# Keeping two PSUM banks open from attention to the end, in a kernel of windowed attention and two expert layers

## The chip, the cores and the metric

One core of one Trainium2 chip. The metric is the time of one execution on the device in microseconds (us); the median over the runs shown is what kernels are compared by.

## What is computed

The reference, cut to what matters (B=2, H=8, S=768, D=64; 4 sinks, window 128; 1536 tokens, model width 512):

```python
scores = scale * np.matmul(q, k.transpose(0, 1, 3, 2))
keep = is_sink | in_window
scores = np.where(keep, scores, -1e9)
a = softmax(scores)
x = np.matmul(a, v)                      # to [1536, 512]
h = x @ w_in                             # d_ff 2048
g = h * np.tanh(softplus(h))
x = g @ w_out
for e in range(4):                       # 4 experts, width 1024
    out += p[:, e:e+1] * (np.maximum(x @ w1[e], 0) @ w2[e])
```

## The kernel before

**Attention.** `banded` runs 24 items (batch, block of 256 queries, pair of heads). An item computes scores `sc` on TensorE, masks and maximises them on VectorE (line 234), exponentiates on ScalarE (238), scales on GpSimd, transposes on TensorE (`tp`, `ts`), and multiplies with `v` (`pv`); `evac_x` (184, 185) writes the result as the pair `xh`, `xl`, whose sum it is.

**Expert layers.** `Experts` cuts each layer's hidden width into units of 512: four units of the first layer (`kind` 0), then two per expert. `stream` goes over units and chunks of tokens. For each chunk `layer1` makes four tiles `h` (f = 0 to 3, 128 hidden values each) of twelve matmuls (four slices of 128 by three products of high and low parts); `mish` turns each into the pair `gh`, `gl`: four steps on ScalarE (552 to 555), then VectorE (556), ScalarE (557), VectorE (558, 559), ScalarE `gh` (89), GpSimd `gl` (97). The bank of `h` is read up to line 559. `layer2` makes four tiles `o` (d = 0 to 3), also of twelve matmuls, copied or added into `acc` (510 to 512). The chunks of the first unit hold 256, 256, 512 and 512 tokens; the last two are called the middle chunk (tokens 512 to 1023) and the last chunk (1024 to 1535) below. A chunk's `layer2` is interleaved with the next chunk's `layer1`.

**Attention and experts overlap.** From the sixth item on (`LAG`) each item is followed by one step of `stream`, and weight parts are converted on VectorE (`split_double`, 116 to 124) beside it. The eight banks of PSUM are dealt out by pools. During attention: one bank for `h`, one for `o`, three for `sc`, two for `tp` and `ts`, one for `pv`. At `first.close()` all eight are given back, and `psum(ctx, 3, 3, 2)` opens three for `h`, three for `o` and two for `r` (an intermediate of `mish`, which lies in `gl` as long as there is no such pool). Which tile was asked for under which pool is fixed by the Python order: the middle chunk's four `h` come from the attention phase's one-bank pool, the last chunk's from the new pool.

**Order.** The order of instructions on each engine is set when the program is built, by a scheduler that looks at dependencies and at free buffers; it does not change at run time, and an engine takes its instructions in that order. In the rows of the order and in the text tiles bear the program's numbers: h_1526, h_1624, h_1794, h_1959 are the middle chunk's f = 0 to 3; h_2099, h_2127, h_2169, h_2211 are the last chunk's in the kernel before, and h_2097, h_2125, h_2167, h_2209 the same four in the changed one. o_2155, o_2197, o_2239, o_2253 (before) and o_2153, o_2195, o_2237, o_2251 (changed) are the middle chunk's outputs. Line numbers from 404 on are larger by up to 11 in the changed kernel: 552 to 559 become 563 to 570, 510 becomes 521, 477 becomes 488, 504 becomes 515.

Of the kernel before, what the change touches and what calls it, by code (L numbers as in the profile page):

```python
# [9 lines left out]
F32 = mybir.dt.float32  # L10
# [5 lines left out]
PSUM = bass.MemoryType.PSUM  # L16

P = 128
# [18 lines left out]
class Ring:  # L37


    def __init__(self, tiles):  # L40
        self.tiles, self.n = tiles, 0
# [52 lines left out]
def split(c, hi, lo, src, eng_hi, eng_lo):  # L94

    copy(c, eng_hi, hi, src)
    eng_lo.tensor_tensor(lo, src, hi.bitcast(F32), ALU.subtract)  # L97
# [67 lines left out]
def banded_masks(c):  # L165

    nc = c.nc
    rel, sink, diag, prev = c.parts
    m0, m1, m2 = c.masks
    nc.vector.tensor_scalar(sink, sink, c.ns, None, ALU.is_ge)  # L170
    nc.vector.scalar_tensor_tensor(diag, rel, c.win, diag, ALU.is_ge, ALU.add)
    nc.vector.scalar_tensor_tensor(m0[:, 0:P], diag, -BIG, sink, ALU.mult, ALU.mult)
    nc.vector.tensor_scalar(prev, rel, float(P), c.win, ALU.add, ALU.is_ge)
    nc.vector.scalar_tensor_tensor(m1[:, 0:P], prev, -BIG, sink, ALU.mult, ALU.mult)
    for m, at, x in ((m1, P, diag), (m2, 0, prev), (m2, P, sink[:, 0:SINKS]), (m2, SEG, diag)):
        nc.gpsimd.tensor_scalar(m[:, at:at + x.shape[1]], x, -BIG, 0.0, ALU.mult, ALU.add)
# [201 lines left out]
class Experts:  # L378
# [5 lines left out]
    def __init__(self, c, ctx):  # L384
        self.c = c
        self.NF = self.FU // P
        self.KT = c.DM // P
        tp = c.tc.tile_pool
        self.acc = c.acc
        self.wpool = [ctx.enter_context(tp(name="m_w0", bufs=1)), None]  # L390
        self.cv = ctx.enter_context(tp(name="m_cv", bufs=1))
        self.tp = ctx.enter_context(tp(name="m_t", bufs=2))
        self.gp = ctx.enter_context(tp(name="m_g", bufs=7))
        self.units = []
        for u in range(c.F1 // self.FU):
            cols = slice(2 * u * self.FU, 2 * (u + 1) * self.FU)
            self.units.append((0, u, c.w_in[:, cols], c.w_out[u * self.FU:(u + 1) * self.FU, :]))
        self.n1 = len(self.units)
        for e in range(c.E):
            for u in range(c.F2 // self.FU):  # L400
                cols = slice(u * self.FU, (u + 1) * self.FU)
                self.units.append((1, e, c.w1[e, :, cols], c.w2[e, cols, :]))
        self.w = {}
        self.parked = {}

    def psum(self, ctx, nh, no, nr=0):
        tp = self.c.tc.tile_pool
        self.pr = ctx.enter_context(tp(name="m_pr", bufs=nr, space=PSUM)) if nr else None
        self.pa = ctx.enter_context(tp(name="m_pa", bufs=nh, space=PSUM))
        self.pb = ctx.enter_context(tp(name="m_pb", bufs=no, space=PSUM))  # L410

    def park(self, pool, n, nm):

# [51 lines left out]
    def layer1(self, n, t0, cw, g):  # L465
        c, nc = self.c, self.c.nc
        kind, e, _, _ = self.units[n]
        NF, KT, n1 = self.NF, self.KT, self.n1
        x = (c.xh, c.xl)
        cols = slice(t0, t0 + cw)  # L470
        wis = self.w[n][0]
        for f in range(NF):
            h = self.pa.tile([P, self.CW], F32, tag="h", name="h")[:, 0:cw]
            fs = slice(f * P, (f + 1) * P)
            for k in range(KT):
                for t, (sw, sx) in enumerate(TERMS):
                    nc.tensor.matmul(  # L477
                        h, lhsT=wis[sw][:, k, fs], rhs=x[sx][:, k, cols],
                        start=k == 0 and t == 0, stop=k == KT - 1 and t == 2,
                    )  # L480
            gh = self.gp.tile([P, self.CW], F32R, tag="gh", name="gh")[:, 0:cw]
            gl = self.gp.tile([P, self.CW], F32R, tag="gl", name="gl")[:, 0:cw]
            if kind == 0:
                self.mish(n, gh, gl, h)
            else:
                nc.scalar.activation(gh, h, AF.Relu)  # L486
                nc.vector.scalar_tensor_tensor(gl, h, 0.0, gh.bitcast(F32), ALU.max, ALU.subtract)  # L487
            g.append((gh, gl))
            yield

    def layer2(self, n, t0, cw, g):
        c, nc = self.c, self.c.nc
        kind, e, _, _ = self.units[n]
        NF, KT, n1 = self.NF, self.KT, self.n1
        cols = slice(t0, t0 + cw)
        wos = self.w[n][1]
        if kind == 0:
            accv = self.acc.rearrange("p (ch d) w -> p ch d w", d=KT)
            for d in range(KT):
                o = self.pb.tile([P, cw], F32, tag="o", name="o")  # L500
                ds = slice(d * P, (d + 1) * P)
                for f in range(NF):
                    for t, (sw, sx) in enumerate(TERMS):
                        nc.tensor.matmul(  # L504
                            o, lhsT=wos[sw][:, f, ds], rhs=g[f][sx],
                            start=f == 0 and t == 0, stop=f == NF - 1 and t == 2,
                        )
                y = accv[:, t0 // c.DM, d, t0 % c.DM:t0 % c.DM + cw]
                if n == 0:
                    nc.scalar.activation(y, o, AF.Copy)  # L510
                else:
                    nc.vector.tensor_tensor(y, y, o, ALU.add)
                if n == n1 - 1:
                    split(c, c.xh[:, d, cols], c.xl[:, d, cols], y, nc.scalar, nc.vector)
                yield
            return
        last = n == len(self.units) - 1
        for d in range(cw // P):
            tt = t0 // P + d
            pcol = c.pn[:, tt, e:e + 1]  # L520
            ds = slice(d * P, (d + 1) * P)
            nw = 2 if last and tt == c.T // P - 1 else 1
            for q in range(nw):
                ms = slice(q * c.DM // nw, (q + 1) * c.DM // nw)
                o = self.pb.tile([P, c.DM], F32, tag="o", name="o")[:, ms]
                for f in range(NF):
                    for t, (sw, sx) in enumerate(TERMS):
                        nc.tensor.matmul(  # L528
                            o, lhsT=g[f][sx][:, ds], rhs=wos[sw][:, f, ms],
                            start=f == 0 and t == 0, stop=f == NF - 1 and t == 2,  # L530
                        )
                y = self.acc[:, tt, ms]
                if n == n1:
                    nc.scalar.activation(y, o, AF.Copy, scale=pcol)
                else:
                    nc.vector.scalar_tensor_tensor(y, o, pcol, y, ALU.mult, ALU.add)  # L536
                if last:
                    nc.sync.dma_start(out=c.out[tt * P:(tt + 1) * P, ms], in_=y)
            yield
# [31 lines left out]
def banded(c, ctx, raws):  # L571

    tc = c.tc
    banded_masks(c)
    first = ExitStack()
    x = Experts(c, ctx)
    w = x.weights(0)
    x.psum(first, 1, 1)
    a = attention_pools(c, first)
    steps = x.stream([(0, 0, QW), (0, QW, QW)] + [(0, t0, x.CW) for t0 in range(2 * QW, c.T, x.CW)] + later(c, x, 1))  # L580
    dram = ctx.enter_context(tc.tile_pool(name="park", bufs=1, space=bass.MemoryType.DRAM))
    w = chain(w, x.park(dram, 1, "wi"), x.park(dram, 1, "wo"), x.park(dram, 2, "wi"), x.park(dram, 2, "wo"))
    items = c.items
    raws = dict(enumerate(raws))
    preps = {}
    done = 0
    for m, it in enumerate(items):
        while done <= min(m + AHEAD, len(items) - 1):
            raw = raws.pop(done) if done in raws else load_item(c, *items[done], pool=a.qk)
            preps[done] = raw, attention_values(c, a, *items[done])  # L590
            done += 1
        attention_item(c, a, *it, preps.pop(m))
        if m < 4 or m in PARK:
            run(w, 1)
        if m >= LAG:
            run(steps, 1)
        if m == 0:
            normalize_probs(c)
    first.close()
    x.wpool[1] = ctx.enter_context(tc.tile_pool(name="m_w1", bufs=1))  # L600
    x.psum(ctx, 3, 3, 2)
    run(x.weights(1))
    run(steps, 4 * (x.NF + 4) - 4 - (len(items) - LAG))
    rest(c, x, steps, 1)


def later(c, x, first):

    return [(n, t0, x.CW) for n in range(first, len(x.units)) for t0 in range(0, c.T, x.CW)]
# [135 lines left out]
```

## Time and profile before

| what | value |
|---|---|
| median of 3 runs | 940.51 us |
| lowest, highest | 940.05, 941.72 us |
| profiled execution | 942.14 us, span in the trace 940.3 us |
| TensorE busy | 915.0 us (97%), 4292 matmuls |
| VectorE, ScalarE, GpSimd busy | 426.6, 349.0, 263.8 us |
| chain that ended last | TensorE 88%, VectorE 8% |

The span is what the trace shows of one execution; the execution's own time is 1.8 us longer. A matmul of 512 columns is listed with a duration of 0.39 us but starts every 0.23 us in a dense row, since matmuls overlap; so distances between starts count. The granted clock is a share of TensorE's full speed.

### The profile page before, as it was taken

Reading aid. Unit: us, or ns where it says so; the run is one execution under the profiler, and the core shown is the slowest. Engines: PE = TensorE matmul, PEld = TensorE weight load, DVE = VectorE, ACT = ScalarE, POOL = GpSimd, SP = SyncE. Lnnn points to the kernel's source line nnn. Section 1 sums busy time; section 2 is a strip of 40 time slices with the busy share of each in tenths; the row PEclk is TensorE's granted clock in tenths of the full one; section 3 lists DMA queues with packets and bytes.
Section 4 is the critical chain, followed back from the end, with each engine's and each line's share of the span. In section 5 each row is a group of like instructions: output and inputs, shape, how many; then the busy total and the mean of one; then the engine's idle time right before and its main releaser. Section 6 shows DMA issues by size and latency. Waiting matters only on the chain.

```text
span 940.3 us, 11148 instructions
## 1 busy us (share of the span) xinstructions
PE 915.0 (97%) x4292; PEld 737.2 (78%) x4292; DVE 426.6 (45%) x770; ACT 349.0 (37%) x745; POOL 263.8 (28%) x217
## 2 busy tenths in 40 slices
PE   7999999879999999999999999999999999999997
PEld 5566767668888888888888888888888888888886
DVE  6899999434589645552112222222222222222222
ACT  4686886378766767732221111111111111111110
POOL 4485665122222355333210220220222122200000
PEclk8798999889999999999999999999999999999999
DMA  7665865722022111011001110110110110000012
GB/s 232 204 216 182 271 224 183 287 90 84 6 90 91 46 45 45 1 45 45 24 22 45 46 43 3 45 45 1 45 45 2 44 45 1 1 1 1 11 45 82
DMA packets 34654, 70.18 MB, mean 75 GB/s; under 512 B 4240, under 2 KB 12688, under 8 KB 34592
## 3 DMA queue, kind: packets, MB, share of 16 engines
q1 hardware_dynamic: 34592, 69.37, 22.3%
q8 instruction: 36, 0.59, 0.3%
q14 instruction: 26, 0.21, 0.1%
HBM read 53.64 MB, written 11.53 MB: 69 GB/s over the span
## 4 chain that ended last, share of the span: by engine, by line
PE 88%; DVE 8%; ACT 1%; DMA 1%; issue 0%; DVEq 0%; ACTq 0%
PE h L477 42%; PE o L528 28%; PE o L504 13%; PE sc L231 2%; DVE pr L234 2%; PE pv L277 2%; PE tp L264 1%; DVE cv_h L119 1%; DVE cv_a L123 1%; DMA stage<-in_moe_w_in_dram 1%; DVE cv_r L122 1%; DVE cv_a L117 1%; PE pv L283 1%; DVE u L556 0%; DVE xl L185 0%; DVE cv_a L121 0%
## 5 line engine op out<-in xcount | busy, mean ns | idle before, releaser
L477 PE MATMUL h<-xh,wih 128*128 128x512 f32 (+1 forms) x592 | 230.3, 389 | 3.9 <-DVE w L559 3.9
L477 PE MATMUL h<-xh,wil 128*128 128x512 f32 (+1 forms) x592 | 228.9, 387 | 0.0
L477 PE MATMUL h<-xl,wih 128*128 128x512 f32 (+1 forms) x592 | 228.1, 387 | 0.0
L486 ACT ACTIVATE gh<-h 128x512 fp32r<-128x512 f32 x96 | 57.4, 598 | 410.1 <-PE h L477 245.2
L487 DVE SCALAR_TENSOR_TENSOR gl<-h,gh 128x512 fp32r<-128x512 f32 x96 | 66.4, 692 | 208.0 <-ACT gh L486 207.9
L528 PE MATMUL o<-wol,gh 128*128 128x512 f32 (+1 forms) x388 | 150.1, 387 | 0.0
L528 PE MATMUL o<-woh,gh 128*128 128x512 f32 (+1 forms) x388 | 150.1, 387 | 0.0
L528 PE MATMUL o<-woh,gl 128*128 128x512 f32 (+1 forms) x388 | 149.9, 387 | 0.0
L536 DVE SCALAR_TENSOR_TENSOR acc<-o,pn,acc 128x512 f32<-128x512 f32 (+1 forms) x85 | 63.3, 745 | 176.2 <-PE o L528 176.2
L477 PEld LDWEIGHTS h<-xh,wih 128*128 128x128 f32 x592 | 112.5, 190 | 28.7 <-DVE w L559 4.5
L477 PEld LDWEIGHTS h<-xh,wil 128*128 128x128 f32 x592 | 112.7, 190 | 22.7 <-DVE mx L234 0.3
L477 PEld LDWEIGHTS h<-xl,wih 128*128 128x128 f32 x592 | 112.3, 190 | 22.6 <-issue 0.6
L97 POOL TENSOR_TENSOR gl<-w,gh 128x512 fp32r<-128x512 f32 (+1 forms) x52 | 67.2, 1294 | 171.3 <-ACT gh L89 161.6
L504 PE MATMUL o<-gh,woh 128*128 128x512 f32 (+1 forms) x208 | 79.9, 384 | 4.9 <-ACT gh L89 4.9
L528 PEld LDWEIGHTS o<-woh,gh 128*128 128x128 f32 x388 | 73.0, 188 | 14.8
L528 PEld LDWEIGHTS o<-woh,gl 128*128 128x128 f32 x388 | 72.9, 188 | 14.9
L528 PEld LDWEIGHTS o<-wol,gh 128*128 128x128 f32 x388 | 72.8, 188 | 14.7
L504 PE MATMUL o<-gh,wol 128*128 128x512 f32 (+1 forms) x208 | 78.6, 378 | 0.0
L504 PE MATMUL o<-gl,woh 128*128 128x512 f32 (+1 forms) x208 | 77.3, 378 | 0.2 <-POOL gl L97 0.2
L87 POOL TENSOR_SCALAR wih<-stage 128x1024 fp32r<-128x1024 f32 x16 | 16.5, 1051 | 190.4 <-PE h L477 190.4
L87 POOL TENSOR_SCALAR woh<-stage 128x1024 fp32r<-128x1024 f32 x16 | 16.5, 1053 | 140.9 <-PE o L528 122.1
L238 ACT ACTIVATE pr<-pr,mx 128x260 f32<-128x260 f32 (+2 forms) x96 | 46.5, 486 | 22.8 <-DVE mx L234 21.7
(87 smaller groups left out, 1102.6 us busy)
## 6 DMA issues: line engine op xcount, KB each, us to landing
stage<-in_moe_w_dram SPq DMA_DIRECT2D x32, 512.0 KB, 3.7
stage<-in_moe_w_in_dram SPq DMA_DIRECT2D x8, 1024.0 KB, 6.6
stage<-in_moe_w_out_dram SPq DMA_DIRECT2D x8, 1024.0 KB, 5.5
qk<-in_qk_dram SPq DMA_DIRECT2D x16, 324.0 KB, 5.2
acc<-in_v_dram SPq DMA_DIRECT2D x16, 192.0 KB, 3.0
out_dram<-acc SPq DMA_DIRECT2D x11, 256.0 KB, 2.0
wih<-cv_h SPq DMA_DIRECT2D x4, 512.0 KB, 3.3
woh<-cv_h SPq DMA_DIRECT2D x4, 512.0 KB, 3.3
```

Source lines behind the costliest of these rows:

```text
L87: eng.tensor_scalar(out, src, 1.0, 0.0, ALU.mult, ALU.add)
L97: eng_lo.tensor_tensor(lo, src, hi.bitcast(F32), ALU.subtract)
L231: nc.tensor.matmul(sc, lhsT=raw[rows, t * P:(t + 1) * P], rhs=raw[rows, k0:k0 + sw], start=True, stop=True)
L234: nc.vector.tensor_tensor_reduce(out=o, in0=sc, in1=c.masks[t if i == 0 else 2][:, 0:sw], scale=-c.scale, scalar=3.0e38, op0=ALU.add, op1= ...
L238: nc.scalar.activation(o, o, AF.Exp, bias=mx[:, e:e + 1], scale=-1.0, accum_out=sm[:, e:e + 1])
L277: nc.tensor.matmul(pv[64 * j:64 * j + 64, q0:q0 + ns * P], lhsT=v[:, blk, j * c.D:(j + 1) * c.D], rhs=pts[j][:, sg:sg + ns], start=n == 0, ...
L477: nc.tensor.matmul(h, lhsT=wis[sw][:, k, fs], rhs=x[sx][:, k, cols], start=k == 0 and t == 0, stop=k == KT - 1 and t == 2,)
L486: nc.scalar.activation(gh, h, AF.Relu)
L487: nc.vector.scalar_tensor_tensor(gl, h, 0.0, gh.bitcast(F32), ALU.max, ALU.subtract)
L504: nc.tensor.matmul(o, lhsT=wos[sw][:, f, ds], rhs=g[f][sx], start=f == 0 and t == 0, stop=f == NF - 1 and t == 2,)
L528: nc.tensor.matmul(o, lhsT=g[f][sx][:, ds], rhs=wos[sw][:, f, ms], start=f == 0 and t == 0, stop=f == NF - 1 and t == 2,)
L536: nc.vector.scalar_tensor_tensor(y, o, pcol, y, ALU.mult, ALU.add)
```

## The change

`psum` no longer replaces the pools of `h` and `o`: it appends to a list of pools per name, one entry per buffer. The attention phase's pools for `h` and `o` are entered on the outer stack and stay open to the end; when attention closes, its six other banks become two `h`, two `o` and two `r` banks. A new method `bank` takes the pool at the head of the list, moves it to the tail and allocates the tile there, so after the switch tiles go in turn over [old, new, new]. All `o` tiles are now 512 columns wide and cut to what is used.

```diff
+        self.banks, self.pr = {}, None
...
     def psum(self, ctx, nh, no, nr=0):
         tp = self.c.tc.tile_pool
-        self.pr = ctx.enter_context(tp(name="m_pr", bufs=nr, space=PSUM)) if nr else None
-        self.pa = ctx.enter_context(tp(name="m_pa", bufs=nh, space=PSUM))
-        self.pb = ctx.enter_context(tp(name="m_pb", bufs=no, space=PSUM))
+
+        k = len(self.banks)
+        if nr:
+            self.pr = ctx.enter_context(tp(name="m_pr", bufs=nr, space=PSUM))
+        for nm, n in (("h", nh), ("o", no)):
+            pool = ctx.enter_context(tp(name=f"m_p{nm}{k}", bufs=n, space=PSUM))
+            self.banks.setdefault(nm, []).extend([pool] * n)
+
+    def bank(self, nm):
+
+        pools = self.banks[nm]
+        pools.append(pools.pop(0))
+        return pools[-1].tile([P, self.CW], F32, tag=nm, name=nm)
...
-            h = self.pa.tile([P, self.CW], F32, tag="h", name="h")[:, 0:cw]
+            h = self.bank("h")[:, 0:cw]
...
-                o = self.pb.tile([P, cw], F32, tag="o", name="o")
+                o = self.bank("o")[:, 0:cw]
...
-                o = self.pb.tile([P, c.DM], F32, tag="o", name="o")[:, ms]
+                o = self.bank("o")[:, ms]
...
-    x.psum(first, 1, 1)
+    x.psum(ctx, 1, 1)
...
-    x.psum(ctx, 3, 3, 2)
+    x.psum(ctx, 2, 2, 2)
```

The order on GpSimd and on the DMA queue is the same in both kernels. On TensorE, in the last items of attention, before (a row is one matmul, written tile first, then what it is made from):

```order
L264 MATMUL tp_1916<-ident_75,pr_1891 128x128 x4
L477 MATMUL h_2099<-xh_94,wih_224 128x512
L477 MATMUL h_2099<-xh_94,wil_225 128x512
L477 MATMUL h_2127<-xh_94,wih_224 128x512
L477 MATMUL h_2127<-xh_94,wil_225 128x512
L477 MATMUL h_2169<-xh_94,wih_224 128x512
L477 MATMUL h_2169<-xh_94,wil_225 128x512
L504 MATMUL o_1707<-gl_1309,woh_350 128x256
L264 MATMUL tp_1923<-ident_75,pr_1891 128x128 x4
```

and in the changed kernel:

```order
L264 MATMUL tp_1916<-ident_75,pr_1891 128x128 x4
L515 MATMUL o_1707<-gl_1309,woh_350 128x256
L264 MATMUL tp_1923<-ident_75,pr_1891 128x128 x4
L277 MATMUL pv_1866<-pt_1854,acc_59 64x256
L277 MATMUL pv_1866<-pt_1861,acc_59 64x256
```

The matmuls of the last chunk that lay between the transposes are gone from here; h_2125 and h_2167 come later, on both sides of h_1624, and h_2097 after h_1959 (next place).

On TensorE behind h_1959, where the last products with the middle chunk's third hidden slice (gl_1808) stand, before:

```order
L504 MATMUL o_2155<-gl_1808,woh_350 128x512
L504 MATMUL o_2197<-gl_1808,woh_350 128x512
L504 MATMUL o_2239<-gl_1808,woh_350 128x512
L504 MATMUL o_2155<-gh_1972,woh_350 128x512
L504 MATMUL o_2155<-gh_1972,wol_351 128x512
```

and in the changed kernel:

```order
L515 MATMUL o_2153<-gl_1808,woh_350 128x512
L515 MATMUL o_2195<-gl_1808,woh_350 128x512
L515 MATMUL o_2237<-gl_1808,woh_350 128x512
L488 MATMUL h_2097<-xh_94,wih_224 128x512
L488 MATMUL h_2097<-xh_94,wil_225 128x512
```

The twelve matmuls of h_2097 have moved between the products of gl_1808 and those of gh_1972 (the fourth slice). After them come nine products of the fourth slice, then the twelve of o_2251, then h_2209.

On ScalarE behind h_1959, before (w, u, r and gl are the steps of `mish`, acc the copies of `o`):

```order
L552 ACTIVATE w_1974<-h_1959 128x512
L552 ACTIVATE w_2114<-h_2099 128x512
L553 ACTIVATE w_1974<-w_1974 128x512
L553 ACTIVATE w_2114<-w_2114 128x512
L554 ACTIVATE u_1975<-w_1974 128x512
L554 ACTIVATE u_2115<-w_2114 128x512
L555 ACTIVATE gl_1973<-u_1975 128x512
L557 ACTIVATE u_1975<-u_1975 128x512
L89 ACTIVATE gh_1972<-w_1974 128x512
```

and in the changed kernel, where the six steps of h_1959 stand alone (lines 563, 564, 565, 566, 568, 89) and from here on:

```order
L563 ACTIVATE w_2112<-h_2097 128x512
L563 ACTIVATE w_2140<-h_2125 128x512
L564 ACTIVATE w_2112<-w_2112 128x512
L564 ACTIVATE w_2140<-w_2140 128x512
L521 ACTIVATE acc_59<-o_2153 128x512
L565 ACTIVATE u_2113<-w_2112 128x512
L521 ACTIVATE acc_59<-o_2195 128x512
L521 ACTIVATE acc_59<-o_2237 128x512
L565 ACTIVATE u_2141<-w_2140 128x512
L566 ACTIVATE r_2114<-u_2113 128x512
L566 ACTIVATE r_2142<-u_2141 128x512
L521 ACTIVATE acc_59<-o_2251 128x512
```

The last chunk's first two tiles now go through the steps side by side, with four copies of `o` between them; lines 568 of both follow. On VectorE the steps of h_1624 (556, 558, 559 before) have moved as well: the first of them stood between two conversion steps (119 and 121), and now stands behind the last one (123).

## Rows read from the trace of the kernel before

**Rows 1.** The page: span, and busy time by engine.

```profile
span 940.3 us, 11148 instructions
PE 915.0 (97%) x4292; PEld 737.2 (78%) x4292; DVE 426.6 (45%) x770; ACT 349.0 (37%) x745; POOL 263.8 (28%) x217
```

**Rows 2.** Waits of TensorE, 147 us to the end: total, times, longest.

```profile
PE o L504 <- ACT gh L89: 4.9, 1, 4.9
PE h L477 <- DVE w L559: 3.6, 1, 3.6
```

**Rows 3.** TensorE by line, 216 us to the end: busy, mean ns, idle before.

```profile
L477 PE MATMUL h<-xh,wih 128*128 128x512 f32 x520 | 202.3, 389 | 0.0
```

**Rows 4.** Busy time by window, 147.10 to 216 us: window, its length, engines, clock, DMA.

```profile
core 0: us, PE busy (x) PEld busy (x) DVE busy (x) ACT busy (x) POOL busy (x), PEclk, DMA share, GB/s
147.10:180.28 33.18, 33.17 (x197) 26.77 (x195) 24.35 (x30) 16.83 (x34) 9.06 (x7) 1.00 0.69 240
180.28:183.88 3.60, 0.00 (x1) 0.00 (x1) 2.08 (x3) 1.28 (x3) 0.00 (x0) 0.92 1.00 408
183.88:190.01 6.13, 6.13 (x14) 4.78 (x15) 0.00 (x0) 1.16 (x3) 1.28 (x1) 0.50 0.05 19
191.80:196.75 4.95, 0.04 (x1) 0.00 (x0) 2.07 (x3) 2.64 (x6) 0.00 (x0) 1.00 0.01 2
196.75:200.50 3.75, 3.75 (x9) 2.95 (x10) 2.07 (x3) 2.93 (x6) 1.28 (x1) 0.54 0.00 0
200.50:216.00 15.50, 15.50 (x70) 12.80 (x69) 7.57 (x11) 14.01 (x26) 5.18 (x4) 1.00 0.43 137
```

**Rows 5.** Timeline of TensorE: start, duration, instruction, [idle before and who ended it].

```profile
150.60 0.48 PE L477 MATMUL h<-xh,wih 128*128 128x512 f32 x1
...
175.35 0.39 PE L477 MATMUL h<-xh,wih 128*128 128x512 f32 x1
...
178.07 0.39 PE L504 MATMUL o<-gh,woh 128*128 128x512 f32 x1
...
183.88 0.79 PE L477 MATMUL h<-xh,wih 128*128 128x512 f32 x1 [3.60 <-DVE w L559]
...
203.27 0.39 PE L504 MATMUL o<-gh,woh 128*128 128x512 f32 x1
```

**Rows 6.** Timeline of VectorE, 166 to 181 us.

```profile
166.20 0.69 DVE L117 TENSOR_SCALAR cv_a<-cv_a 128x1024 f32<-128x1024 f32 x1 [1.18 <-ACT cv_a L116]
...
168.80 0.68 DVE L556 SCALAR_TENSOR_TENSOR u<-w,gl 128x512 f32<-128x512 f32 x1
169.40 0.69 DVE L121 TENSOR_SCALAR cv_a<-cv_h 128x1024 int32<-128x1024 int32 x1
...
170.94 1.22 DVE L123 SCALAR_TENSOR_TENSOR cv_a<-stage,cv_a 128x1024 f32<-128x1024 uint32 x1
172.07 0.68 DVE L558 SCALAR_TENSOR_TENSOR u<-u,gl 128x512 f32<-128x512 f32 x1
...
180.95 0.69 DVE L556 SCALAR_TENSOR_TENSOR u<-w,gl 128x512 f32<-128x512 f32 x1 [7.40 <-ACT gl L555]
```

**Rows 7.** Timeline of ScalarE, 178 to 196 us.

```profile
178.33 0.60 ACT L552 ACTIVATE w<-h 128x512 f32<-128x512 f32 x1 [4.12 <-PE h L477]
...
189.46 1.09 ACT L552 ACTIVATE w<-h 128x512 f32<-128x512 f32 x2 [4.97 <-PE h L477]
190.43 1.15 ACT L553 ACTIVATE w<-w 128x512 f32<-128x512 f32 x2
191.47 1.15 ACT L554 ACTIVATE u<-w 128x512 f32<-128x512 f32 x2
192.51 0.62 ACT L555 ACTIVATE gl<-u 128x512 fp32r<-128x512 f32 x1
193.89 0.63 ACT L557 ACTIVATE u<-u 128x512 f32<-128x512 f32 x1 [0.76 <-DVE u L556]
...
196.07 0.63 ACT L89 ACTIVATE gh<-w 128x512 fp32r<-128x512 f32 x1 [1.55 <-DVE w L559]
```

## The prediction

> **What bounds the kernel now.** I read the page first. TensorE (PE) is busy 97% of the 940.3 us span [rows 1], so the end moves only when PE idles, or runs at the lower of its two clocks, for longer or shorter; PE's work itself is not touched by this change. Next the waits of TensorE from 147 us to the end: only two are left, 4.9 us for a `gh` of ScalarE (line 89) and 3.6 us for a `w` of VectorE (line 559) [rows 2]. After 216 us PE has no idle time at all [rows 3]. So the stretch that matters is 147 to 216 us, the end of attention and the hand-over to the experts, and the table of windows cuts it up [rows 4]: dense to 180.28; 3.60 us still; 6.13 us at a granted clock of 0.50 (the 1.2 GHz level) for 14 matmuls; after a short dense piece 4.95 us still; 3.75 us at 0.54 for 9 matmuls; dense from 200.50 on. Each time PE had been idle just before the clock was low.
>
> Why it stands still: the middle chunk's four `h` tiles (h_1526, h_1624, h_1794, h_1959) share one bank, since that pool has one buffer. Each may start only when the chain on the one before it is done: four ScalarE steps, line 556, 557, 558, 559. From the end of h_1794's twelve matmuls (178.07, where the next matmul starts) to the first one of h_1959 (183.88) are 5.81 us [rows 5]. PE hides this as long as it has filler. Before, the filler is the last chunk: its h_2099, h_2127 and h_2169 lie in the three banks of the scores, free early, and run from 150.60 on [rows 5]; by 175.35 all 36 matmuls of them are done.
>
> **The change, part by part.** Pools and slices add no instruction: every engine issues the same operations, POOL and SP in the same order too, so nothing is paid or saved in work. What moves is which bank a tile gets. `bank` takes the pool at the head of [old, new, new] and puts it at the tail. The last chunk's first tile (h_2097, called h_2099 before) therefore gets the old bank, **behind h_1959 in the same serial chain**; f=1 and f=2 get two new ones, and f=3 (h_2209) the old one again, behind h_2097. `r` now takes two banks of the scores, which is early, but the order on ScalarE uses it only after h_1959's steps. The `o` list turns likewise, so the middle chunk's fourth output (o_2251) comes back to the bank of the first.
>
> *Up to h_1794.* The filler goes: one tile (12 matmuls) fewer stands ahead of h_1794, and the others come later. Twelve matmuls take 178.07 − 175.35 = 2.72 us [rows 5]. In their place VectorE sets the time: line 556 of h_1624 (one between 168.80 and 169.40, so 0.60) now stands behind the last weight conversion, which ended at 172.07 [rows 6]; without it ahead 171.47. From line 556 to the next `h` takes 183.88 − 180.95 = 2.93 [rows 5, 6]. h_1794 starts at 171.47 + 2.93 = 174.40, not 175.35. PE alone would be there at 175.35 − 2.72 = 172.63, so it idles some 1.8 us in between, in pieces under 1 us as I place them. The row nearest to such pieces is the dense stretch at clock 1.00 [rows 4], so I charge no clock here; the other end is one low stretch more (below).
>
> *Stop 1, h_1959.* 174.40 + 2.72 + 5.81 = 182.93. PE has only nine `o` matmuls meanwhile (9 × 0.2275 = 2.05), and idles 3.76 us: the old 3.60 again.
>
> *Stop 2, h_2097, new.* The old order gave PE nine `o` matmuls that wait for `gh` (the 4.9 us); the new one puts h_2097 there, waiting for the bank. Since ScalarE does no steps of another tile between (the old order ran two tiles side by side, [rows 7]), 5.81 holds: 182.93 + 2.72 + 5.81 = 191.46, again 3.76 us idle.
>
> *Stop 3, h_2209, new.* It waits for h_2097's chain, and that one is long: twelve ScalarE instructions stand from its line-563 step up to its line-568 step, among them f=1's and four copies of `o`. Six such took 192.51 − 189.46 = 3.05, so 0.51 each [rows 7]; twelve are 6.1, with 0.26 from PE to ScalarE (178.07 to 178.33, [rows 5, 7]) 6.4. Line 557 to a free bank is 196.07 − 193.89 = 2.18 [rows 7], and up to 0.6 more because two tiles go through VectorE together: 8.6 to 9.2, I take 8.9. h_2209 starts at 191.46 + 2.72 + 8.9 = 203.08. PE has 21 `o` matmuls in there (4.78) and idles 4.1 us. At full clock h_2209 ends at 205.80, with 12 matmuls more behind it (o_2251) than the old kernel had at 203.27, when its h_2211 ended [rows 5]: 205.80 − 2.72 − 203.27 = **−0.2 us**. So at full clock the longer chain is just paid by the fill that no longer comes first.
>
> *The clock.* The two stops of before fell to 1.2 GHz. They cost 6.13 − 14 × 0.2275 = 2.9, and 3.75 − 9 × 0.2275 = 1.7 us [rows 4]; both are inside 203.27. The three stops of after are as long, and each is followed by an `h` tile that the chain waits for. A stop costs from 1.7 (nine slow matmuls) to 12 × (0.438 − 0.2275) = 2.5 (6.13 / 14 = 0.438 each, all twelve slow). I take 1.8, near the lower row, since of the two low stretches that one was over before twelve matmuls were through. 3 × 1.8 = 5.4. Sum: −0.2 + 5.4 = **+5.2 us**. Beyond 216 us nothing idled [rows 3], and with three `h`, three `o` and two `r` banks in both kernels I cost the rest at nothing; if that cover went, each further stop would cost its idle time and 1.7 to 2.5 us.
>
> The Trainium skill (Perfetto Trace Analysis, Optimizing Tensor Performance) says that independent matmul groups should rotate through different PSUM banks, so that emptying one overlaps the next group; it speaks for this change, which adds rotation. The rows agree with its reason (the one-bank pool is what PE waits for), not with the gain: the turn begins on the one bank still in use. By the rule taken at its word the sum would be that of the third rival, below.
>
> **The rivals.** *The clock holds* in all or two of the three new stops. For it: the lull at 191.80 to 196.75 itself shows 1.00, the fall came only with the work behind it [rows 4]; and VectorE's conversions stood 1.18 us for a ScalarE copy [rows 6], which is 1.2 us off h_1794's start if that wait goes in the new order. Against it: both stops of 3.6 us and more fell. Sum: −0.2 − 1.2 = −1.4, to −0.2 + 1.8 = +1.6 us. That is not slower by what can be told; the place is the first matmuls of h_1959, h_2097 and h_2209, and it decides when at most one of the three runs at 1.2 GHz.
>
> *A fourth stop:* the 1.8 us ahead of h_1794 come in one piece and drop the clock, or all three stops cost the full 2.5. −0.2 + 4 × 1.8 = +7.0; with 2.5 each +9.8 us. For it: VectorE is behind all along there. Against: PE has two `o` tiles, attention's products and two `h` tiles left to spread.
>
> *The rotation does free PE:* h_2097 and h_2209 find a bank in time, so stops 2 and 3 go, with 3.76 + 4.1 us of idle time and two low stretches: −0.2 + 1.8 − 7.9 = −6.3, so 934.2 us. Against it: `bank` and the new order put h_2097 straight behind h_1959's chain, and the order on each engine is fixed.
>
> **How the numbers follow.** The profiled execution took 942.1 us (span 940.3), the three runs have a median of 940.5; the difference of 5.2 is put on the median: **945.7 us**. About 0.2%, 1.9 us, is what a measurement of this kernel can tell from no change. Chances: the forecast (two or three low stretches, +3.4 to +7.3) 0.72; the clock holds 0.15; a fourth stop 0.09; rotation frees PE 0.04. Range: from the upper end of the clock rival (+1.6, so 942.1) to the fourth stop with dear stretches (+9.8, so 950.3). It leaves out most of the clock rival and the rotation. Slower is 0.72 + 0.09 = 0.81, with 0.01 of the clock rival 0.82; the same 0.13 from the clock rival; faster 0.04, with 0.01 of the clock rival 0.05.
>
> **What would show it.** In the profile after: three stops of PE between 177 and 206 us, for line 570 (559 before), of 3.5 to 4.2 us each, ahead of h_1959, h_2097 and h_2209; granted clock near 0.5 behind at least two of them; no wait of 4.9 us for `gh`; the fill at 150 us gone; dense PE from some 209 us on. A line-89 wait of 4 us or more, or dense PE between 191 and 203 us, would prove the order read wrongly; full clock behind the stops would prove the clock term wrong; idle time beyond 216 us would mean that the banks' new turn costs something later, which I cost at nothing.

## The result, and the profile after

The changed kernel is **slower**: 947.57 us, median of ten runs (943.56 to 949.59), beside 940.40 us for ten runs of the kernel before (936.41 to 943.44). The ratio is 1.0071 with a 95% interval of 1.0050 to 1.0093, which on 940.4 us is +6.7 us (+4.7 to +8.7). The ratio goes by all runs; the two medians lie 7.2 us apart. Forecast were 945.7 us, +5.2, with a range of 942.1 to 950.3. The profiled execution took 949.59 us, the longest of the ten and 7.4 more than that of the kernel before.

The page of the changed kernel, against [rows 1]:

```profile
span 947.7 us, 11150 instructions
...
PE 920.0 (97%) x4292; PEld 739.6 (78%) x4292; DVE 425.4 (45%) x770; ACT 349.0 (37%) x745; POOL 262.9 (28%) x217
```

Every engine is listed with as many instructions as before (the total is larger by two), and all but TensorE (PE, PEld) are busy for the same time within 1.2 us. TensorE's 5 us more are for the same 4292 matmuls: they took longer, and the windows below show the lower clock that goes with it. The rest of the loss is waiting. TensorE's waits from 140 us to the end, which answer to [rows 2]:

```profile
PE h L488 <- DVE w L570: 10.7, 4, 3.6
PE o L515 <- ACT acc L521: 1.1, 2, 0.7
```

The wait of 4.9 us for `gh` is gone. In its place the wait for line 570 (559 before), which was there once with 3.6 us, now comes four times with 10.7 us. Beyond 216 us there is still nothing, as in [rows 3]; one of TensorE's rows by line, which all end in 0.0:

```profile
L488 PE MATMUL h<-xh,wih 128*128 128x512 f32 x524 | 203.8, 389 | 0.0
```

The timeline of TensorE shows the places. The matmuls are the first of h_1526, h_1794, h_1959, h_2097, o_2251, h_2209 and of the next `h`:

```profile
146.15 0.80 PE L488 MATMUL h<-xh,wih 128*128 128x512 f32 x1
...
175.69 0.50 PE L488 MATMUL h<-xh,wih 128*128 128x512 f32 x1 [0.35 <-DVE w L570]
...
184.36 0.80 PE L488 MATMUL h<-xh,wih 128*128 128x512 f32 x1 [3.60 <-DVE w L570]
...
195.49 0.50 PE L488 MATMUL h<-xh,wih 128*128 128x512 f32 x1 [3.58 <-DVE w L570]
...
202.85 0.50 PE L515 MATMUL o<-gh,woh 128*128 128x512 f32 x1 [0.69 <-ACT acc L521]
...
208.99 0.50 PE L488 MATMUL h<-xh,wih 128*128 128x512 f32 x1 [3.12 <-DVE w L570]
...
213.24 0.58 PE L488 MATMUL h<-xh,wih 128*128 128x512 f32 x1
```

There are three stops of over 3 us, ahead of the three tiles that share the old bank with the tile before them. The table of windows over the same stretch, columns as in [rows 4]:

```profile
146.15:151.43 5.28, 5.28 (x13) 4.13 (x13) 5.28 (x5) 0.53 (x2) 3.99 (x4) 0.50 0.25 102
151.43:175.69 24.26, 23.55 (x152) 18.66 (x150) 18.80 (x24) 13.15 (x27) 1.48 (x1) 0.98 0.67 197
...
180.76:184.36 3.60, 0.00 (x1) 0.00 (x1) 2.07 (x3) 1.28 (x3) 0.00 (x0) 0.80 1.02 413
184.36:189.64 5.28, 5.28 (x12) 4.17 (x13) 0.00 (x0) 0.61 (x1) 1.27 (x1) 0.50 0.27 108
...
191.91:195.49 3.58, 0.00 (x2) 0.00 (x1) 2.07 (x3) 1.27 (x3) 0.00 (x0) 1.00 0.00 0
195.49:199.88 4.39, 4.39 (x12) 3.48 (x13) 0.00 (x0) 0.61 (x1) 1.28 (x1) 0.62 0.00 0
...
205.87:208.99 3.12, 0.00 (x1) 0.00 (x1) 2.69 (x6) 1.65 (x4) 0.00 (x0) 1.00 0.00 0
208.99:213.24 4.25, 4.25 (x12) 3.38 (x13) 0.54 (x1) 3.36 (x6) 2.52 (x2) 0.64 0.01 4
```

Behind each stop the granted clock is 0.50 to 0.64, and the twelve matmuls of an `h`, which take 2.72 us at full clock [rows 5], take 5.28, 4.39 and 4.25 us. That is 2.56 + 1.67 + 1.53 = 5.8 us. The lag against the kernel before can be read at one point of the program, as the prediction did: h_2209 ends at 213.24, with the twelve matmuls of o_2251 (2.72) behind it that the old kernel did later, so 213.24 − 2.72 − 203.27 = 7.25 us [rows 5]. The two spans differ by 7.4, so the whole loss lies ahead of 213 us.

### The profile page after: what moved, and what is told of

Same layout as the page of the kernel before. It is cut to its first block, busy times and chain, and to the rows that moved or that the text cites. A ratio compares the mean times of both kernels' runs of the same rounds, so it can differ in the third digit from the quotient of the medians.

```text
span 947.7 us, 11150 instructions
## 1 busy us (share of the span) xinstructions
PE 920.0 (97%) x4292; PEld 739.6 (78%) x4292; DVE 425.4 (45%) x770; ACT 349.0 (37%) x745; POOL 262.9 (28%) x217
## 4 chain that ended last, share of the span: by engine, by line
PE 87%; DVE 8%; ACT 2%; DMA 1%; issue 0%; POOL 0%; ACTq 0%; DVEq 0%
PE h L488 42%; PE o L539 28%; PE o L515 13%; PE sc L231 2%; PE pv L277 2%; DVE pr L234 2%; PE tp L264 1%; DMA stage<-in_moe_w_in_dram 1%; DVE cv_a L123 1%; DVE cv_r L122 1%; DVE cv_h L119 1%; DVE cv_a L117 1%; PE pv L283 1%; DVE cv_a L121 0%; DVE u L569 0%
## 5 line engine op out<-in xcount | busy, mean ns | idle before, releaser
L488 PE MATMUL h<-xl,wih 128*128 128x512 f32 (+1 forms) x592 | 231.1, 390 | 0.0
```

The source lines that it names most:

```text
L488: nc.tensor.matmul(h, lhsT=wis[sw][:, k, fs], rhs=x[sx][:, k, cols], start=k == 0 and t == 0, stop=k == KT - 1 and t == 2,)
```

## The experiments

Differences in us are a line's ratio less one, times 941; the ratio is that of all runs (5 to 12 of each kernel), not of the medians. All are compared with the kernel before on the same chip.

| kernel | median us | ratio to before | 95% interval | difference |
|---|---|---|---|---|
| changed | 947.57 | 1.0071 | 1.0050–1.0093 | +6.7 |
| e1 new banks first | 944.38 | 1.0031 | 1.0010–1.0053 | +2.9 |
| e2 `h`, `o` pools opened first | 944.20 | 1.0039 | 1.0018–1.0060 | +3.7 |
| e8 both | 941.86 | 1.0016 | 0.9991–1.0041 | +1.5 |
| e3 only `o` stays open | 943.08 | 1.0028 | 1.0006–1.0050 | +2.6 |
| e9 only `h` stays open | 944.36 | 1.0044 | 1.0023–1.0066 | +4.1 |
| e4 changed, stops filled | 942.53 | 1.0017 | 0.9995–1.0038 | +1.6 |
| e5 before, stops filled | 940.13 | 0.9988 | 0.9964–1.0011 | −1.1 |
| e6 before, 13 steps | 936.65 | 0.9953 | 0.9932–0.9974 | −4.4 |
| e12 the same again | 936.72 | 0.9944 | 0.9924–0.9964 | −5.3 |
| e7 changed, 13 steps | 931.75 | 0.9904 | 0.9869–0.9940 | −9.0 |
| e11 the same again | 932.45 | 0.9898 | 0.9865–0.9931 | −9.6 |
| e10 changed, 13 steps, new first | 930.22 | 0.9888 | 0.9856–0.9920 | −10.5 |

**e4 and e5: the clock by itself.** Twelve matmuls with weights of zero, added into an open `o` group, stand in each stop; they leave every value as it is. e4 is the changed kernel with three such fills, e5 the kernel before with the first two.

```diff
                     for t, (sw, sx) in enumerate(TERMS):
+                        if t == 2 and n == 0 and t0 == 2 * QW and (d, f) in ((2, 1), (2, 2), (3, 3)):
+                            for _ in range(12):
+                                nc.tensor.matmul(o[0:P // 2], lhsT=c.zero, rhs=g[f][0], start=False, stop=False, skip_group_check=True)
                         nc.tensor.matmul(
...
+    c.zero = c.const.tile([P, P // 2], F32R, name="zero")
+    nc.gpsimd.memset(c.zero.bitcast(F32), 0.0)
```

> The changed kernel with three times twelve matmuls by a tile of zeros (64 of 128 rows, 512 columns, added into an open group of o, so the result stays) that lie in the three stops, before h_1959, h_2097 and h_2209; 36 x 0.23 = 8.2 us of PE work that fills idle time of 3.60, 3.58 and 3.12 us up to some 0.9 us each. If the clock's fall behind a stop is what costs 1.5 to 2.5 us each: no low stretch behind the three, 4.5 to 6 us faster than the changed kernel, so +1 to +2.5 us against the kernel before. If the clock costs nothing on this path (the chain of ScalarE and VectorE sets the time): unchanged, +6 to +8 us.

> The kernel before with twice twelve matmuls by zeros in its two stops (before h_1959, and before the products of the fourth slice that wait for gh). If the clock behind a stop costs what its profile showed (2.9 and 1.7 us) and the chain is otherwise the same: 3 to 4.6 us faster than the kernel before, span some 936 to 937 us, and the two kernels with filled stops differ by the chain alone, the changed one +4 to +6 us slower. If filling helped the changed kernel for another reason (not the clock): no change here, within 1.5 us.

The changed kernel came down from +6.7 to +1.6 us, with 36 matmuls more. Its timeline of TensorE, with the first matmuls of h_1794, h_1959, h_2097 and h_2209:

```profile
174.43 0.50 PE L488 MATMUL h<-xh,wih 128*128 128x512 f32 x1 [0.40 <-DVE w L573]
...
183.10 0.50 PE L488 MATMUL h<-xh,wih 128*128 128x512 f32 x1 [0.83 <-DVE w L573]
...
191.76 0.50 PE L488 MATMUL h<-xh,wih 128*128 128x512 f32 x1 [0.83 <-DVE w L573]
...
203.36 0.50 PE L488 MATMUL h<-xh,wih 128*128 128x512 f32 x1
```

and five of its windows, the last two around and behind the third stop:

```profile
147.20:174.43 27.23, 26.11 (x164) 20.66 (x163) 24.73 (x30) 13.87 (x30) 6.43 (x5) 1.00 0.63 197
...
180.00:188.00 8.00, 7.17 (x31) 5.07 (x30) 2.08 (x3) 3.12 (x6) 1.29 (x1) 1.00 0.57 229
188.00:194.00 6.00, 5.17 (x23) 3.49 (x22) 2.07 (x3) 2.04 (x4) 1.30 (x1) 1.00 0.00 0
194.00:204.00 10.00, 9.25 (x40) 6.35 (x39) 3.77 (x6) 7.50 (x15) 0.00 (x0) 1.00 0.01 2
204.00:220.00 16.00, 16.00 (x72) 13.26 (x71) 5.33 (x9) 12.98 (x23) 5.14 (x4) 1.00 0.38 132
```

The fills don't free a bank: the four tiles start at 174.43, 183.10, 191.76 and 203.36, beside 174.40, 182.93, 191.46 and 203.08 in the prediction's working, which had no clock in it yet. Only the clock is different, 1.00 throughout. So the chain is as long as it was worked out, and 5.1 us of the 6.7 are the clock, as the expectation of a falling clock had it; what is left, +1.6, is known to −0.5 to +3.6.

e5 is a **miss**: −1.1 us instead of −3 to −4.6. Its waits:

```profile
PE o L507 <- ACT gh L89: 2.6, 1, 2.6
PE h L477 <- DVE w L562: 1.9, 2, 1.0
```

2.6 of the 4.9 us for `gh` are still a stop that the fill does not cover; the interval (−3.4 to +1.0) touches the expectation. Its trace shows where the rest went. From the first matmul of h_1526 to the end of h_2211 pass 194.81 − 140.95 = 53.86 us, beside 203.27 − 147.15 = 56.12 in the kernel before, so 2.3 less. The stretch behind the first stop gave back 2.4 of its 2.9: from the first matmul of h_1959 to the first product with gh_1972 are 188.55 − 178.11 = 10.44 us instead of 12.87. The second gave back only 0.4 of its 1.7 (from there to h_2211 3.39 us instead of 3.75), since h_2211 now waits for its bank, which it did not before:

```profile
191.94 0.50 PE L477 MATMUL h<-xh,wih 128*128 128x512 f32 x1 [1.04 <-DVE w L562]
```

(The span of its profiled execution, 931.7 us, is not to be used: TensorE's clock was 0.93 in its first 47 us where the other kernels' mostly have 0.78, so the medians and this one stretch are compared.) Between the two filled kernels lie 2.7 us in the runs, not the 4 to 6 that were expected, with intervals that overlap. In the traces e4 takes 206.21 − 2.72 − 147.24 = 56.25 us for the same stretch (o_2251 taken off as above), 2.4 more than e5. That is the price of the longer chain alone, with the clock out of it on both sides.

**e1: the turn begins with the new banks.** In place of appending the new pools to the list:

```diff
-            self.banks.setdefault(nm, []).extend([pool] * n)
+            self.banks[nm] = [pool] * n + self.banks.get(nm, [])
```

> The two new banks are put ahead of the old one in the turn, nothing else: the last chunk's f=0 and f=1 take new banks, f=2 the old one, f=3 the bank of f=0. Theory A (the loss is the old bank at the head of the turn, which chains h_2097 behind h_1959 and h_2209 behind h_2097): stop 3 goes (3.12 us idle and some 1.5 us of low clock in the profile of the changed kernel), stop 2 becomes the wait before f=2, with a low stretch; so about +7 - 4.6 = +1 to +3.5 us against the kernel before, and two long stops in the trace instead of three. Theory B (the loss is the late fill and VectorE's later conversion steps ahead of h_1794): those stay as they are, +6 to +8 us. Rival C (clock alone): +7 less 1.5 for each low stretch that is gone.

Measured +2.9, 3.8 less than the changed kernel. The last chunk's first two tiles now lie in new banks and only f = 2 takes the old one: there are two stops instead of three, in the timeline of TensorE

```profile
184.02 0.79 PE L488 MATMUL h<-xh,wih 128*128 128x512 f32 x1 [3.61 <-DVE w L570]
...
195.76 0.79 PE L488 MATMUL h<-xh,wih 128*128 128x512 f32 x1 [5.10 <-DVE w L570]
```

That is within theory A's +1 to +3.5; rival C's sum, some +5.5 with one low stretch gone, lies outside the interval (+0.9 to +5.0). So which tile meets the bank in use makes part of the cost, but not all; the second stop has become longer.

**e2: the `h` and `o` pools are opened before `r`.** The new `h` banks are then others of the six, among them ones that come free earlier, and `r` takes later ones.

```diff
         k = len(self.banks)
-        if nr:
-            self.pr = ctx.enter_context(tp(name="m_pr", bufs=nr, space=PSUM))
         for nm, n in (("h", nh), ("o", no)):
             pool = ctx.enter_context(tp(name=f"m_p{nm}{k}", bufs=n, space=PSUM))
             self.banks.setdefault(nm, []).extend([pool] * n)
+        if nr:
+            self.pr = ctx.enter_context(tp(name="m_pr", bufs=nr, space=PSUM))
```

> When attention closes, the h pool is opened ahead of the r pool, so the new h banks are two of the scores' (early) and r takes one of the scores' and one of the transposes'; the turn is that of the changed kernel, old bank first. The fill of h_2125 and h_2167 comes back among the transposes. Theory A: the three stops before h_1959, h_2097 and h_2209 stay, +4 to +7 us against the kernel before. Theory B: the fill is what was lost, so within 2 us of the kernel before.

Measured +3.7: under A's 4 to 7 by a little, over B's 2, and by its interval (+1.7 to +5.6) it could be either; the trace decides. The last chunk's tiles that have new banks run between the transposes again, yet the two stops of 3.60 us stay, since the chain through the old bank does. But the clock did not fall behind the first of them. The windows behind the two stops:

```profile
182.29:187.30 5.01, 5.00 (x21) 3.86 (x21) 0.00 (x0) 2.44 (x4) 1.28 (x1) 1.00 0.38 151
...
190.94:197.50 6.56, 6.55 (x21) 4.96 (x21) 0.00 (x0) 2.56 (x5) 1.27 (x1) 0.75 0.00 1
```

In the first 21 matmuls take 5.01 us at 1.00; in the second as many take 6.56.

**e8: e1 and e2 together.**

> Both repairs of the change together: new banks first in the turn, and the h pool opened ahead of r (early banks, fill among the transposes). Theories A and B together leave nothing of the loss but the stop before f=2: the two repairs alone gave +2.9 and +3.7 us of +6.7, so 3.8 and 3.0 less; if they add, within 1.5 us of the kernel before. If they mend the same thing: +2 to +4 us.

+1.5 us, no longer told apart from the kernel before. The two repairs take 3.8 and 3.0 us off and together 5.2, so by these figures they add up for the most part; the interval (−0.8 to +3.9) does not exclude that they mend partly the same thing.

**e3 and e9: one of the two names alone.** e3 closes the first `h` pool with attention and opens three (`psum(ctx, 3, 2, 2)`), so that only `o` stays open; e9 does the same for `o` (`psum(ctx, 2, 3, 2)`), so that only `h` stays. The core of e9's edit (`short` is the attention phase's own stack):

```diff
-            pool = ctx.enter_context(tp(name=f"m_p{nm}{k}", bufs=n, space=PSUM))
+            on = short if short and nm == "o" else ctx
+            pool = on.enter_context(tp(name=f"m_p{nm}{k}", bufs=n, space=PSUM))
+            if nm == "o":
+                self.banks[nm] = []
...
-    x.psum(ctx, 1, 1)
+    x.psum(ctx, 1, 1, short=first)
...
-    x.psum(ctx, 2, 2, 2)
+    x.psum(ctx, 2, 3, 2)
```

> Only the o bank stays open (three o banks in turn, old first); the h pool is closed with attention and three new h banks are opened, in other places than before (one of the scores', two of the transposes' and products'), so the fill comes late. Theory A: no new stop, the two of the kernel before (3.6 us before h_1959, about 5 us for gh) with their low clock: 0 to +2 us. Theory B: late fill, late h_1794: +5 to +8 us.

> Only the h bank stays open; o gets three new banks at the switch, as before. Theory A (the first h of the last chunk falls on the bank still in use, and that makes the three stops): the stops of 3.6 us ahead of h_1959 and of the last chunk's first tile come back, each with low clock behind it, and the time is +3 to +6 us over the kernel before; with the +2.6 us of keeping only o it would then about add up to the +6.7 us of the change. Rival B (h and o cost something only together): within 1.5 us of before.

`o` alone costs +2.6, a little over theory A's 0 to +2, and `h` alone +4.1, as theory A had it but for the clock, which held behind its second stop (last section). Their sum is the +6.7 of the change, but each is known to ±2 us only, and neither run changes one thing alone: the new `h` banks lie elsewhere too, so that the fill comes late in e3 and is back among the transposes in e9 (from 150.80 us on). e9 has the chain back in its waits (TensorE from 100 us on),

```profile
PE h L491 <- DVE w L573: 8.9, 4, 3.6
PE o L518 <- ACT acc L524: 1.2, 1, 1.2
```

where e3 has the two stops of the kernel before [rows 2], one of them longer:

```profile
PE o L518 <- ACT gh L89: 5.3, 1, 5.3
PE h L491 <- DVE w L573: 3.6, 1, 3.6
```

In e3's profiled execution h_1794 starts 2.05 us later than in the kernel before (175.35), and without a wait:

```profile
177.40 0.39 PE L491 MATMUL h<-xh,wih 128*128 128x512 f32 x1
```

1.28 us of that are there when h_1526 ends (151.29 beside 150.01), whose matmuls ran at 0.61; the other 0.77 come after it, where matmuls of the last chunk stand ahead of h_1794. How much of the 2.6 us this is in other executions is not shown; the interval reaches from +0.6 to +4.7.

**e6, e7, e10 to e12: the switch comes earlier for the experts.** Only 13 of the 19 steps are asked for beside attention, the other six after the switch. The scheduler may still run them between the last items, but their tiles come from the pools opened at the switch: the middle chunk's f = 1 to 3 no longer all share the one old bank. The same edit in both kernels (e10 has e1's edit as well):

```diff
-        if m >= LAG:
+        if LAG <= m < LAG + 13:
...
-    run(steps, 4 * (x.NF + 4) - 4 - (len(items) - LAG))
+    run(steps, 4 * (x.NF + 4) - 4 - 13)
```

> The kernel before, but only 13 steps of the stream run beside attention in place of 19 (the last six items have none), so of the middle chunk only f=0 is asked for under the one-bank pool; f=1 to 3 and all later tiles come from the three-bank pool. If the one-bank chain is what makes PE stop after attention (theory A at its root): no wait of 3 us or more between 150 and 220 us, both low stretches gone; two stops of 3.6 and 4.9 us and 4.6 us of clock make 13 us at most, less what attention loses as filler (six steps, some 12 us of PE work, come later): 4 to 10 us faster than the kernel before. If attention needed those steps as filler: PE idles among the last items, and the time is within 3 us of the kernel before or above.

> The same 13 steps in the changed kernel: h still goes over [old, new, new], but the old bank is asked for by fewer tiles in a row (f=0, then f=1 of the middle chunk). Theory A: with the one-bank chain gone at its root, keeping the banks costs little: 0 to 4 us slower than the kernel before with 13 steps, and faster than the kernel before. If keeping the banks costs for another reason: still 5 to 8 us slower than that one.

> The changed kernel with 13 steps once more, beside the kernel before with 13 steps on the same chip. Theory A (keeping the banks is a gain of 3 to 6 us where the switch comes early): -7 to -11 us against before, and 3 to 6 us below its neighbour. Rival B (the first five times of it were low by chance): within 1.5 us of its neighbour, so some -4.5 us against before.

> The kernel before with 13 steps once more, as the neighbour of the run above. Both theories: -3 to -6 us against before; what counts is the distance to the run above (A: 3 to 6 us, B: at most 1.5 us).

The kernel before gained 4.4 and 5.3 us by it, which was expected. The changed kernel gained some 16 and became the faster of the two, by 4.3 us in the second pair (932.45 against 936.72) and 4.9 in the first. That is a **miss in sign** of e7's expectation and held when repeated (theory A of e11). The waits of TensorE from 100 us on in the changed kernel with 13 steps (e11):

```profile
PE h L488 <- DVE w L570: 1.9, 2, 1.6
PE sc L231 <- DVE mx L234: 0.7, 1, 0.7
```

and in the kernel before with 13 steps (e12):

```profile
PE pv L277 <- DVE xl L185: 2.3, 3, 1.8
PE o L504 <- DVE xl L185: 1.8, 1, 1.8
PE sc L231 <- DVE mx L234: 1.6, 3, 0.9
```

Neither has a stop of 3 us any more: the chain through the one bank is nearly gone from both. What TensorE waits for in the kernel before are now attention's own results on VectorE (lines 185 and 234), 5.7 of the 6.5 us in that list; in the changed kernel such waits are 0.7 of 3.6 (each list's groups of under 0.7 us are left out here). The same stretch in windows, e11 and then e12:

```profile
164.00:188.00 24.00, 22.23 (x116) 17.87 (x115) 15.11 (x21) 15.71 (x29) 3.90 (x4) 1.00 0.78 285
188.00:216.00 28.00, 28.00 (x126) 23.19 (x125) 10.45 (x16) 22.86 (x41) 7.75 (x6) 1.00 0.23 76
```

```profile
164.00:188.00 24.00, 21.57 (x131) 18.12 (x130) 17.06 (x25) 17.60 (x36) 5.49 (x4) 0.93 0.85 301
188.00:216.00 28.00, 28.00 (x125) 23.21 (x124) 11.43 (x17) 21.58 (x38) 7.23 (x6) 1.00 0.23 76
```

Both are dense from 188 us on; the difference is made before. The waits differ by 2.9 us and the two spans by 5.4. What the rest is stays open: e12's clock was 0.93 in its first window, but 1.00 in e6, the same kernel. That a kept bank is what spares those waits (a tile in it need not wait until attention returns its banks) fits, but no run separates it from the rest of the order, which differs too.

> The changed kernel with 13 steps beside attention and the new banks at the head of the turn. Theory A (with the switch after 13 steps the chain is covered by other matmuls, so that the order of the turn no longer matters): within 2 us of the changed kernel with 13 steps (-7 to -11 us against before). Rival B (the turn still costs something there): a further 2 to 4 us faster, as new first gave 3.7 us at the late switch.

e10 is theory A's case: −10.5, 0.9 us from e11. Where the chain through the old bank is down to 1.9 us of waits, the order of the turn makes no difference that can be told. It has the lowest median of all kernels here, some 10 us under the kernel before.

## Why the prediction was right

**The direction, the mechanism and the places were right.** h_2097 and h_2209 went behind the chain of the old bank, the wait for `gh` made room for them, and three stops came at the three places named. By its steps, read from the profiled execution:

- *No work added, nothing after 216 us.* Held.
- *Up to h_1794.* The order on VectorE did what was said: line 567 of h_1624 stands right behind the last conversion, and from there to h_1794 are 175.69 − 172.76 = 2.93 us, the forecast figure. Timeline of VectorE, after:

```profile
166.81 0.69 DVE L117 TENSOR_SCALAR cv_a<-cv_a 128x1024 f32<-128x1024 f32 x1 [1.19 <-ACT cv_a L116]
...
171.63 1.22 DVE L123 SCALAR_TENSOR_TENSOR cv_a<-stage,cv_a 128x1024 f32<-128x1024 uint32 x1
172.76 0.69 DVE L567 SCALAR_TENSOR_TENSOR u<-w,gl 128x512 f32<-128x512 f32 x1
```

  But h_1794 came at 175.69 instead of 174.40, **+1.3 us**. In this execution h_1526's twelve matmuls ran at 0.50 (146.15 to 151.43, 5.28 us), a stretch ahead of the first matmul that the change moves; in e4, with the same order on TensorE but for the fills, they ran at 1.00, and h_1794 started at 174.43. So this 1.3 us belongs to the execution rather than to the change, as far as two traces can show it. VectorE's wait of 1.18 us for ScalarE [rows 6], which one rival let go, stayed (1.19).
- *Stops 1 and 2.* From the end of a tile to the next 5.80 and 5.85 us, forecast 5.81. *Stop 3:* 9.11, forecast 8.9 (8.6 to 9.2). Its idle time came in two pieces: 0.69 us ahead of o_2251, which had to wait for the bank of the first output, and 3.12 ahead of h_2209; that is 3.81 of the forecast 4.1, and why this stop is shorter than the 3.5 to 4.2 us named as its sign. The prediction named that bank's return and gave it no price; inside the longer wait it cost nothing.
- *At full clock −0.2 us.* e4 is this case: +1.6 in the runs (−0.5 to +3.6), +0.2 in the span, +0.1 from h_1526 on (56.25 beside 56.12).
- *The clock.* Forecast 3 × 1.8 = 5.4; measured 2.56 + 1.67 + 1.53 = 5.8 in the profile, and 5.1 by filling the stops.

**What was off is sizes.** Together the terms miss by 7.25 − 5.2 = 2.0 us in the profiled execution: h_1794's start 1.3, the twelve matmuls of h_1794 0.15, the clock 0.4, stop 3 0.2. In the runs the miss is 1.5 us, within the interval. The term most at fault as the prediction put it is "I charge no clock here" for the stretch up to h_1794: there was a low stretch, though not behind the pieces of idle time that it spoke of (they came to 24.26 − 23.55 = 0.71 us, and in e4 to 1.12, not 1.8), and so its price belongs to no step.

Of the rivals, *the clock holds* was not met by the changed kernel's profile; e2 shows it behind one of three stops, so its chance of 0.15 was not idle. *A fourth stop* did not come. *The rotation frees PE* did not come either: the turn began with the one bank still in use. The Trainium skill (Perfetto Trace Analysis, Optimizing Tensor Performance) has the rule behind this rival, that independent matmul groups should rotate through different PSUM banks. The runs bear it out only in part. With the turn and the places of the banks mended (e8) the added rotation costs nothing that can be told, and gains nothing either (−0.8 to +3.9 us). With the switch after 13 steps (e11) the changed kernel is 4.3 us under its own comparison. So the first bank of the turn and the places of the new ones decided most of the loss, and the moment of the switch decided its sign.

## What to carry to other kernels

When tiles rotate over banks of which one is still in use, look at which tile gets that one: with a fixed order on the engine, the tile that waits for it holds up all that stand behind it. Here the matmuls of h_2125 and h_2167 in the two new banks were done before 175 us, and TensorE still stood 3.58 us for the old one. Price a stop of TensorE with what follows it: here three stops with 10.3 us of idle time cost 5 us more through the clock, and a filler of useless matmuls got that back; the same filler was worth only 1.1 us in the kernel before. Before judging a way to share buffers, move the moment of the hand-over: the same change cost 6.7 us with 19 steps ahead of it and was worth 4 to 5 with 13.

## What was not expected of the hardware

The fall of the clock behind a stop is not certain. After idle stretches of 3.60, 3.58 and 3.12 us the changed kernel ran at 0.50, 0.62 and 0.64, but e2 ran at 1.00 behind 3.60 us (above), e8 likewise behind 3.60 us (21 matmuls in 4.99 us), and e9 behind its second stop, of 3.19 us. Its windows, each stop's follower:

```profile
184.23:189.50 5.27, 5.27 (x12) 4.15 (x13) 0.00 (x0) 0.61 (x1) 1.27 (x1) 0.50 0.02 10
...
195.36:199.80 4.44, 4.44 (x19) 3.68 (x20) 0.00 (x0) 1.94 (x4) 1.28 (x1) 1.00 0.00 0
```

Shorter stops can be followed by the lower clock too. In e2 the last chunk's f = 3 comes after two waits of 1.21 and 1.87 us, with the twelve matmuls of the middle chunk's fourth output between them:

```profile
198.73 0.50 PE L515 MATMUL o<-gh,woh 128*128 128x512 f32 x1 [1.21 <-ACT acc L521]
...
203.61 0.50 PE L488 MATMUL h<-xh,wih 128*128 128x512 f32 x1 [1.87 <-DVE w L570]
```

Its twelve matmuls took 4.46 us (203.61 to 208.07, clock 0.62), as dear as those behind 3.58 us. e9 shows the same behind 1.24 and 1.84 us.

The length of the stop alone does not tell these apart, and what does stays open. For a forecast this means a price of 0 to 2.6 us for each stop of over 3 us, with 1.5 to 2.6 in all three of the changed kernel's profile.
